# A planner that gives out shared PSUM banks when an operation begins, and counts changes between whole and tiled matmuls

## The chip, the cores and the metric

The kernel runs on one core of a Trainium2 chip. The metric is device time in microseconds (us) from launch to end; a lower number is better. A time of a kernel is the median of several runs, and a profile is one further execution in which every instruction has its start and its duration.

## The reference

```python
def _attn_ref(q, k, v, p):                     # 8 batches, 8 heads, 576 tokens, width 64
    scale = 1.0 / np.sqrt(q.shape[-1])
    def sm_attn(qq, kk, vv):
        s = scale * np.matmul(qq, kk.transpose(0, 1, 3, 2))
        s = s - np.max(s, axis=-1, keepdims=True)
        a = np.exp(s)
        a = a / (np.sum(a, axis=-1, keepdims=True) + 1e-09)
        return np.matmul(a, vv)
    p_packed = sm_attn(p, k, v)                # 32 packed rows for each head
    return sm_attn(q, p_packed, p_packed)
...
x = attn_out.transpose(0, 2, 1, 3).reshape(4608, 512)
h = x @ w_in                                   # 512 x 1024
sm = softmax(h);  solu = h * sm
ln = (solu - mean) / np.sqrt(var + 1e-06) * g_ln
x = ln @ w_out                                 # 1024 x 512
h = x @ w_in2                                  # 512 x 2048
return np.maximum(h, 0.0) ** 2 @ w_out2        # 2048 x 512
```

## The kernel before

The program has four stages, and the engines overlap them. The **attention stage** works through 16 units, numbered 0 to 15: one unit is four heads of one batch. For a unit, k and q are loaded (tiles `kr`, `qr`, which share one buffer), transposed on DVE (`kT`, `qT`), and laid out anew by DMA inside SBUF (`k2`, `q2`; units 0 to 3 use `kT` as it is). On PE a unit makes the scores of the packed rows (`s1_mm`, two halves), the transposes of their exponentials (`pt_tr`), the packed values (`pp_mm`), a transpose of these (`pp_tr`), the scores of q against them (`s2_mm`, two halves) and the product of the packed values with the first layer's input weights (`g_mm`, two halves, tile `G`). DVE, ACT and GpSimd (POOL) do maxima, exponentials, sums and copies between these steps.

The **first layer** takes 36 tiles of 128 tokens: `h` is built from `aT` (the transposed second softmax) and `G` of the batch's two units, in four steps, the softmax and norm follow on DVE, ACT and POOL, PE transposes the result (`tr`, banks `ptv`) and multiplies it with the output weights (`y_mm`, operations in two halves of 12 matmuls). The weights come in as raw double precision and are decoded on ACT, DVE and POOL while the first units run: four tiles `wi`, then four tiles `wx` that end as `wo`. The **z** and **o** stages are the second layer, whose two products are made with fewer multiplications by sums and differences of blocks; their weights are decoded and stored during the stages ahead of them (`prepare`).

All work is written down as operations with their engine, a guessed duration, the buffers they read and write, and a first urgency. A **planner** (class `Plan`) then sets the order in which each engine issues its instructions. It runs the operations through a simple model of the chip (`order`): an operation that has its inputs is *ready*, and a free engine takes the ready operation with the smallest urgency. Then `backward` runs the order from its end to its beginning and replaces each urgency by the latest time at which the operation may start. Eight such passes are made, and the last order is the program. PE, DVE, ACT, POOL and the DMA queue each carry out their list strictly in that order. Some operations may go to either of two engines, and the planner chooses (the last step of decoding, L503, is one of them).

Eight banks of PSUM exist. Four of them, the ring `m` that `bank()` hands out, are shared by every short product: scores, transposes, `pg`, `py`, and later `pw`, `pz` and `pa`. In the kernel before, `claim` gives an operation its bank as soon as it is ready, in the order in which operations become ready; an operation that finds no bank free is put into the ring's queue, and is made ready anew when a bank is returned. So a ready operation of low urgency that PE will not take for a long time holds a bank meanwhile. The planner gives each matmul operation a duration that does not depend on its neighbour.

A matmul is called *whole* here when it uses all 128 rows and columns of the array, and *tiled* when it uses 64 of the rows or columns and two or four run side by side: `s1_mm` from unit 4 on, `pp_mm`, `s2_mm`, `g_mm` (L543, L667, L713).

Of the kernel before, what the change touches and what calls it, by code (L numbers as in the profile page):

```python
# [40 lines left out]
class Ring:  # L41


    def __init__(self, tag, bufs, shared):
        self.tag, self.bufs, self.shared = tag, bufs, shared
        self.last, self.free, self.queue = [], list(range(bufs)), []
# [35 lines left out]
class Op:  # L82


    def __init__(self, engines, urgency, fn, lag, bufs, deps, port):
        self.engines, self.urgency, self.fn, self.lag, self.bufs, self.deps = engines, round(urgency, 6), fn, lag, bufs, deps
        self.port = port
        self.engine = None


class Plan:
# [5 lines left out]
    WINDOW = 3413.0  # L97

# [50 lines left out]
    def reset(self):  # L149
        for o in self.ops:  # L150
            o.engine = None
            for b in o.bufs:
                b.slot = None
                if b.ring:
                    b.ring.free, b.ring.queue = list(range(b.ring.bufs)), []

    def backward(self):
# [47 lines left out]
    def order(self):  # L205
# [7 lines left out]
        events = []  # L213
# [25 lines left out]
        order = []  # L239

        def claim(i):
            need = [b for b in ops[i].bufs if b.ring and b.ring.shared and b.slot is None]
            for n, b in enumerate(need):
                if len(b.ring.free) <= sum(c.ring is b.ring for c in need[:n]):
                    b.ring.queue.append((ops[i].urgency, i))
                    return False
            for b in need:
                b.slot = b.ring.free.pop(0)
            return True

        def take(e, t):
            nonlocal port
            while not busy[e] and able[e]:
                _, i = heapq.heappop(able[e])
                o = ops[i]
                if o.engine is not None:
                    continue
# [3 lines left out]
                if e == POOL or e == DVE and o.port:  # L261
                    port = self.span = max(t, port) + o.engines[e]
                else:
                    self.span = pe_end(t, o.engines[e]) if e == PE else t + o.engines[e]
                self.ends[i] = self.span
                heapq.heappush(events, (self.span, i, "free"))
                heapq.heappush(events, (self.span + o.lag, i, "done"))

        while events:
            now = events[0][0]  # L270
            while events and events[0][0] <= now:
                t, i, what = heapq.heappop(events)
                o = ops[i]
                if what == "ready":
                    if claim(i):
                        for e in o.engines:
                            heapq.heappush(able[e], (o.urgency, i))
                elif what == "free":
                    busy[o.engine] = False
                else:  # L280
                    for b in o.bufs:
                        uses[b] -= 1
                        if not uses[b] and b.slot is not None:
                            b.ring.free.append(b.slot)
                            for _, j in sorted(b.ring.queue):
                                heapq.heappush(events, (t + 200, j, "ready"))
                            b.ring.queue.clear()
# [4 lines left out]
            for e in (PE, ACT, POOL, DVE, DMA):  # L292
                take(e, now)
        assert len(order) == len(ops), "the plan is stuck"
# [15 lines left out]
def kernel(  # L310
# [46 lines left out]
    PASSES = 8  # L357
    SUB, KLO, ALO = (POOL,), (DVE,), (POOL,)
# [198 lines left out]
    def pack(at, b, g):  # L557
# [61 lines left out]
        for hf in range(2):  # L619
# [8 lines left out]
            plan.op(PE, c_prod(2, SH, True) if early else PAIR, at + 4, s1_mm, r=[pb, ks], w=[ps])  # L628
            plan.op(DVE, c_dve(SH), at + 5, lambda ps=ps, hf=hf: nc.vector.tensor_reduce(
# [40 lines left out]
        plan.op(PE, KJ * 280 + 60, at + 10, pp_mm, r=[eT, vr], w=[ppp])  # L670

# [20 lines left out]
    def unpack(at, b, g, packed):  # L692
# [3 lines left out]
        for hf in range(2):  # L696
# [4 lines left out]
            plan.op(PE, PAIR, at, s2_mm, r=[ppq, qs], w=[s2])  # L701
            plan.op(DVE, c_dve(SH), at + 1, lambda s2=s2, bs=slice(hf * NB // 2, (hf + 1) * NB // 2): nc.vector.transpose(
# [3 lines left out]
        for f in range(F1 // 512):  # L706
# [7 lines left out]
            plan.op(PE, 957, at + GA, g_mm, r=[ppq, wi[2 * g], wi[2 * g + 1]], w=[pg], claim=[gt])  # L714
            hi_op(at + GA + 1, 512, lambda fs=fs: gt()[:, 0, fs], pg, [pg], [gt])
# [539 lines left out]
```

## Time and profile before

| what | us |
|---|---|
| median of 3 runs | 1254.61 |
| lowest and highest of them | 1252.86, 1256.75 |
| span of the profiled execution | 1251.4 |
| PE busy in that span | 1201.0 (96%) |
| DVE, ACT, POOL busy | 894.0, 785.4, 205.3 |

For the profiled execution the span from the first to the last instruction is the only time shown; it lies 3.2 us below the median of the runs. Matmuls overlap each other by a little, so a busy PE can hide small gaps, and the start of a matmul tells more than its duration. "Idle before" names the time that an engine sat idle and what ended it.

### The profile page before, as it was taken

How to read it: one execution, taken by the hardware profiler on the slowest of the kernel's cores; microseconds unless marked ns; L12 is line 12 of the kernel's file. 1: busy time of each engine (PE TensorE's matmuls, PEld its weight loads, DVE VectorE, ACT ScalarE, POOL GpSimd, SP SyncE). 2: the span in 40 equal slices, each digit the busy share in tenths (PEclk: the TensorE clock that was granted, in tenths of full speed). 3: DMA queues.
4: the chain of work that ended last, by engine and by line, in shares of the span. 5: the costliest groups of instructions: out<-in, count | busy, mean ns of one | idle time of the engine just before them, and what ended most of it. 6: DMA issues, size and time to landing. Idle time of an engine off the chain costs nothing.

```text
span 1251.4 us, 23307 instructions
## 1 busy us (share of the span) xinstructions
PE 1201.0 (96%) x8332; PEld 1097.0 (88%) x8332; DVE 894.0 (71%) x1756; ACT 785.4 (63%) x1669; POOL 205.3 (16%) x250
## 2 busy tenths in 40 slices
PE   3769999999999999999999999999999999999998
PEld 2337887788877789999999999999999999999998
DVE  5897768575867765355686867582778797878885
ACT  2476757575856667478777877787655554545452
POOL 2274534434344442000000000000000000000000
PEclk9989999999999999999999999999999999999999
DMA  8964765765677628656867576746996535343501
GB/s 193 244 177 126 198 197 151 214 175 160 183 214 188 183 81 314 225 194 202 259 191 242 172 257 203 225 156 203 375 352 202 150 117 152 116 150 104 173 31 51
DMA packets 185240, 234.60 MB, mean 187 GB/s; under 512 B 24356, under 2 KB 148772, under 8 KB 184356
## 3 DMA queue, kind: packets, MB, share of 16 engines
q1 hardware_dynamic: 144708, 208.20, 54.4%
q10 hardware_dynamic: 40416, 24.91, 6.6%
q8 instruction: 65, 1.06, 0.4%
q14 instruction: 51, 0.42, 0.1%
HBM read 130.55 MB, written 85.98 MB: 173 GB/s over the span
## 4 chain that ended last, share of the span: by engine, by line
PE 84%; DMA 7%; DVE 4%; POOL 2%; ACT 1%; issue 1%; SPq 1%; DVEq 0%; POOLq 0%; ACTq 0%
PE px L469 10%; PE px L471 10%; PE px L470 10%; PE ph L784 7%; PE pa L469 5%; PE pa L471 5%; PE pa L470 5%; PE py L469 4%; PE py L470 4%; PE py L471 4%; PE pz L470 3%; PE pz L471 3%; PE pz L469 3%; PE ptv L827 2%; PE s L543 2%; PE pg L713 2%
## 5 line engine op out<-in xcount | busy, mean ns | idle before, releaser
L451 ACT CAST cb<-ga 128x384 fp32r<-128x384 f32 x336 | 168.3, 513 | 164.2 <-PE px L471 72.8
L454 DVE TENSOR_TENSOR cb<-ga,cb 128x384 fp32r<-128x384 f32 x336 | 181.2, 555 | 59.1 <-ACT cb L451 58.0
L469 PE MATMUL py<-v,wo 128*128 128x256 f32 x576 | 169.2, 294 | 0.7 <-DVE G L454 0.3
L470 PE MATMUL py<-v,wo 128*128 128x256 f32 x576 | 162.7, 282 | 0.0
L471 PE MATMUL py<-v,wo 128*128 128x256 f32 x576 | 162.6, 282 | 0.0
L469 PE MATMUL px<-oi,cb 128*128 128x256 f32 x504 | 142.3, 282 | 2.0 <-ACT cb L451 2.0
L471 PE MATMUL px<-oi,cb 128*128 128x256 f32 x504 | 142.0, 282 | 0.1
L470 PE MATMUL px<-oi,cb 128*128 128x256 f32 x504 | 141.8, 281 | 0.0
L469 PE MATMUL pa<-oi,cb 128*128 128x256 f32 x504 | 141.4, 281 | 0.0
L471 PE MATMUL pa<-oi,cb 128*128 128x256 f32 x504 | 141.0, 280 | 0.0
L470 PE MATMUL pa<-oi,cb 128*128 128x256 f32 x504 | 141.0, 280 | 0.0
L469 PE MATMUL px<-y,zi 128*128 128x384 f32 x384 | 129.4, 337 | 0.0
L470 PE MATMUL px<-y,zi 128*128 128x384 f32 x384 | 129.4, 337 | 0.0
L471 PE MATMUL px<-y,zi 128*128 128x384 f32 x384 | 129.3, 337 | 0.0
L469 PEld LDWEIGHTS py<-v,wo 128*128 128x128 f32 x576 | 109.7, 191 | 13.1 <-issue 9.4
L470 PEld LDWEIGHTS py<-v,wo 128*128 128x128 f32 x576 | 110.0, 191 | 0.6
L471 PEld LDWEIGHTS py<-v,wo 128*128 128x128 f32 x576 | 109.8, 191 | 0.0
L1032 DVE TENSOR_TENSOR gw<-pz,gw 128x384 f32<-128x384 f32 x96 | 53.2, 554 | 73.3 <-PE pz L471 64.0
L972 DVE TENSOR_TENSOR ga<-ga 128x384 f32<-128x384 f32 x192 | 100.4, 552 | 0.9
L469 PEld LDWEIGHTS px<-oi,cb 128*128 128x128 f32 x504 | 95.9, 190 | 2.2 <-ACT cb L451 2.2
L471 PEld LDWEIGHTS px<-oi,cb 128*128 128x128 f32 x504 | 96.0, 190 | 0.3 <-DVE cb L454 0.3
L470 PEld LDWEIGHTS px<-oi,cb 128*128 128x128 f32 x504 | 95.6, 190 | 0.0
(179 smaller groups left out, 2972.6 us busy)
## 6 DMA issues: line engine op xcount, KB each, us to landing
g_dram<-gw SPq DMA_DIRECT2D x192, 192.0 KB
ga<-g_dram SPq DMA_DIRECT2D x96, 384.0 KB
zi<-z_dram SPq DMA_DIRECT2D x28, 512.0 KB
oi<-o_dram SPq DMA_DIRECT2D x24, 512.0 KB
kr<-in_k_dram SPq DMA_DIRECT2D x16, 576.0 KB
qr<-in_q_dram SPq DMA_DIRECT2D x16, 576.0 KB
q<-qT SPq DMA_DIRECT2D x64, 144.0 KB
y_dram<-ysb ACTq DMA_DIRECT2D x72, 128.0 KB
```

Of the source, the lines that this page charges most:

```text
L451: plan.op(ACT, c_act(cols, sbuf=r[0].pool not in (psm, psh, pso)), at, lambda: nc.scalar.copy(out_(), in_()), r=r, w=w)
L454: plan.either(on(cols, *engines), at, lambda e: vec[e].tensor_tensor(out_(), in_(), hi_().bitcast(F32), op=ALU.subtract), r=r, w=w, port=i ...
L469: nc.tensor.matmul(ps, lh, rh, start=first, stop=False, skip_group_check=onto)
L470: nc.tensor.matmul(ps, lh, rl, start=False, stop=False, skip_group_check=onto)
L471: nc.tensor.matmul(ps, ll, rh, start=False, stop=last, skip_group_check=onto)
L543: nc.tensor.matmul(ps()[64 * e:64 * e + 64, :SH], cols(lhs, e), cols(rhs, e)[:, cs], start=True, stop=True)
L713: nc.tensor.matmul(pg()[es, :], ppq()[:, e], wi[2 * g + e]()[:, fs], start=True, stop=True)
L784: nc.tensor.matmul(ph()[:, fs], al[l]()[:, g], g_tiles[b, g]()[:, r, fs], start=ends[0] and g == 0 and t == 0, stop=ends[1] and g == NG - ...
L827: nc.tensor.transpose(pt()[:, c * P:(c + 1) * P], e()[:, (4 * t + c) * P:(4 * t + c + 1) * P], ident)
L972: plan.op(DVE, c_dve(cols), at, lambda: nc.vector.tensor_tensor(out_(), in0(), in1(), op=op), r=r, w=w, port=True)
L1032: plan.op(DVE, c_dve(HN), when(p, SN), lambda: nc.vector.tensor_tensor(t(), ps()[:, :HN], t(), op=ALU.add), r=[t, ps], w=[t])
```

## The change

The instructions are the same; the planner that orders them differs in four ways. A bank of the shared ring is now claimed when PE begins the operation (`claim` is called in `take`), so a ready operation holds nothing. If an operation cannot get its banks, the engine looks at the next one by urgency, and what it would have needed is held back from less urgent ones. A bank that is returned counts as free 200 ns later. And the model of PE adds 90 ns when a tiled operation follows a whole one, and 200 ns when a whole one follows a tiled one (`SWITCH`; `tiled` marks the operations). A field `slack`, which would make operations earlier in the backward pass, is added but stays 0, and `AHEAD` is not read.

```diff
+        self.slack, self.tiled = 0, False
...
+    SWITCH = {True: 90.0, False: 200.0}
...
-                    free[j] = max(free[j], t + self.hop(ops[j].engine, e) + ops[j].lag)
+                    free[j] = max(free[j], t + self.hop(ops[j].engine, e) + ops[j].lag + ops[j].slack)
...
-        def claim(i):
-            need = [b for b in ops[i].bufs if b.ring and b.ring.shared and b.slot is None]
-            for n, b in enumerate(need):
-                if len(b.ring.free) <= sum(c.ring is b.ring for c in need[:n]):
-                    b.ring.queue.append((ops[i].urgency, i))
+        mode = [False]
+
+        def claim(i, held, now):
+            need = {}
+            for b in ops[i].bufs:
+                if b.ring and b.ring.shared and b.slot is None:
+                    need.setdefault(b.ring, []).append(b)
+            for ring, bufs in need.items():
+                if sum(f <= now for f, _ in ring.free) - held.get(ring, 0) < len(bufs):
+                    for r, bs in need.items():
+                        held[r] = held.get(r, 0) + len(bs)
                     return False
...
+                if not claim(i, held if keep else {}, t):
+                    back.append(item)
+                    continue
...
+                elif e == PE:
+                    ns = o.engines[e]
+                    if o.tiled != mode[0]:
+                        ns += self.SWITCH[o.tiled]
+                        mode[0] = o.tiled
+                    self.span = pe_end(t, ns)
...
                 if what == "ready":
-                    if claim(i):
-                        for e in o.engines:
-                            heapq.heappush(able[e], (o.urgency, i))
+                    for e in o.engines:
+                        heapq.heappush(able[e], (o.urgency, i))
...
-                            b.ring.free.append(b.slot)
-                            for _, j in sorted(b.ring.queue):
-                                heapq.heappush(events, (t + 200, j, "ready"))
-                            b.ring.queue.clear()
+                            b.ring.free.append((t + 200, b.slot))
+                            heapq.heappush(events, (t + 200, i, "wake"))
...
+            plan.ops[-1].tiled = not early
```

The order moves from the first microseconds to the end of the first layer; in the z stage a few neighbours change places, and in the o stage the order of PE is the same. The lines of the changed file are 24 to 28 higher (L543 becomes L567, L784 becomes L812). Three places show it.

On **PE**, at unit 5, where the scores of q (`s<-q`) and the product with the weights (`pg`) stand between the steps of `h` (`ph`), the order before is:

```order
392 L827 MATMUL ptv<-ident,e 128x128 x4
393 L543 MATMUL s_1669<-q_1265,ppq 64x288 x2
394 L543 MATMUL s_1676<-q_1265,ppq 64x288 x2
395 L784 MATMUL ph<-G,ah 128x512 x4
396 L784 MATMUL ph<-G,al 128x512 x2
397 L543 MATMUL s_1696<-k_1432,pbz_752 64x288 x2
398 L713 MATMUL pg<-wi_327,ppq 64x512
399 L713 MATMUL pg<-wi_364,ppq 64x512
400 L784 MATMUL ph<-G,ah 128x512 x4
401 L784 MATMUL ph<-G,al 128x512 x2
```

and the order after:

```order
186 L812 MATMUL ph<-G,ah 128x512 x4
187 L812 MATMUL ph<-G,al 128x512 x2
188 L567 MATMUL s_1252<-q_1031,ppq 64x288 x2
189 L567 MATMUL s_1261<-q_1031,ppq 64x288 x2
190 L740 MATMUL pg<-wi_322,ppq 64x512
191 L740 MATMUL pg<-wi_367,ppq 64x512
192 L740 MATMUL pg<-wi_322,ppq 64x512
193 L740 MATMUL pg<-wi_367,ppq 64x512
194 L812 MATMUL ph<-G,ah 128x512 x4
195 L812 MATMUL ph<-G,al 128x512 x2
```

Here the four tiled operations of the unit stand in one run between whole ones, where before they stood in two runs, with the unit's other `pg` pair in a third further down.

On **PE**, at unit 3 (scores `s<-kT`, their transposes `pt`), while the weights are still being decoded, the order before is:

```order
38 L543 MATMUL s_547<-q_459,ppq 64x288 x2
39 L625 MATMUL s_559<-kT,pbz_142 128x288 x2
40 L761 MATMUL ph<-G,aT 128x512 x2
41 L625 MATMUL s_576<-kT,pbz_142 128x288 x2
42 L761 MATMUL ph<-G,aT 128x512 x2
43 L653 MATMUL pt<-ident,e_608 128x128 x4
44 L653 MATMUL pt<-ident,e_608 64x128
```

and the order after:

```order
38 L789 MATMUL ph<-G,aT 128x512 x2
39 L649 MATMUL s_565<-kT,pbz_142 128x288 x2
40 L649 MATMUL s_573<-kT,pbz_142 128x288 x2
41 L740 MATMUL pg<-wi_207,ppq 64x512
42 L740 MATMUL pg<-wi_222,ppq 64x512
43 L789 MATMUL ph<-G,aT 128x512 x4
44 L678 MATMUL pt<-ident,e_621 128x128 x4
45 L678 MATMUL pt<-ident,e_621 64x128
```

Between the unit's last score and its transposes there stood one step of `ph`, and now there stand an operation of `pg` and two steps of `ph`; both scores come in a row.

On **DVE**, at the decoding of the first `wx` and the attention of unit 1 (`d_504`, `d_456` are its row sums, `pp` is unit 2's), the order before is:

```order
61 L500 SCALAR_TENSOR_TENSOR wraw<-wraw 128x1024
62 L644 TENSOR_SCALAR rs<-sm 128x1
63 L503 TENSOR_TENSOR wx<-wx,wraw 128x1024
64 L646 RECIPROCAL rs<-rs 128x1
65 L726 TENSOR_REDUCE d_504<-a_443 128x18
66 L673 SCALAR_TENSOR_TENSOR pp<-ppp,rs,mask 128x256
67 L728 TENSOR_SCALAR d_504<-d_504 128x18
68 L495 SCALAR_TENSOR_TENSOR wx<-wx,wraw 128x1024
69 L729 RECIPROCAL d_504<-d_504 128x18
```

and the order after:

```order
61 L519 SCALAR_TENSOR_TENSOR wx<-wx,wraw 128x1024
62 L754 TENSOR_REDUCE d_456<-a_410 128x18
63 L669 TENSOR_SCALAR rs<-sm 128x1
64 L522 TENSOR_SCALAR wraw<-wx 128x1024
65 L756 TENSOR_SCALAR d_456<-d_456 128x18
66 L671 RECIPROCAL rs<-rs 128x1
67 L524 SCALAR_TENSOR_TENSOR wraw<-wraw 128x1024
68 L757 RECIPROCAL d_456<-d_456 128x18
69 L606 STREAM_TRANSPOSE pbz_142<-pr 32x2x32 x3
70 L699 SCALAR_TENSOR_TENSOR pp<-ppp,rs,mask 128x256
```

The `TENSOR_TENSOR wx<-wx,wraw` of L503 is no longer in DVE's list; it is POOL's now, which carries it out ahead of its multiplication with `g_neg`. The transposes for `pbz`, which stood earlier, come later.

## Rows read from the trace of the kernel before

**Rows 1.** The page: busy us, share of the span, instructions of each engine.

```profile
PE 1201.0 (96%) x8332; PEld 1097.0 (88%) x8332; DVE 894.0 (71%) x1756; ACT 785.4 (63%) x1669; POOL 205.3 (16%) x250
```

**Rows 2.** Busy time by stretch: us, engines' busy us (instructions), PE clock, DMA share, GB/s.

```profile
0.00:100.00 100.00, 59.19 (x248) 29.78 (x249) 79.55 (x130) 48.86 (x92) 41.30 (x44) 0.95 0.80 204
100.00:520.00 420.00, 417.14 (x2963) 344.01 (x2961) 288.69 (x550) 279.01 (x609) 164.05 (x206) 1.00 0.63 183
520.00:885.00 365.00, 364.29 (x2099) 363.46 (x2099) 232.54 (x459) 274.69 (x578) 0.00 (x0) 1.00 0.67 215
885.00:892.00 7.00, 4.87 (x28) 4.46 (x27) 5.59 (x12) 3.91 (x9) 0.00 (x0) 0.81 1.03 382
892.00:1247.00 355.00, 355.00 (x3001) 355.00 (x3001) 287.21 (x606) 178.88 (x383) 0.00 (x0) 1.00 0.49 158
```

**Rows 3.** What PE waited for: us in total, times, the longest.

```profile
PE s L625 <- DVE pbz L582: 10.4, 1, 10.4
PE ptp L683 <- DVE pp L673: 8.9, 2, 5.3
PE pt L653 <- ACT e L640: 8.6, 4, 3.8
```

**Rows 4.** Timeline of PE around tiled products: start us, us, line, operation, count.

```profile
161.08 0.28 PE L470 MATMUL py<-v,wo 128*128 128x256 f32 x1
161.20 0.28 PE L471 MATMUL py<-v,wo 128*128 128x256 f32 x1
161.41 1.46 PE L667 MATMUL ppp<-vr,eT 128*64 128x128 f32 x20
...
204.66 0.71 PE L543 MATMUL s<-k,pbz 128*64 128x288 f32 x4
205.19 1.03 PE L713 MATMUL pg<-wi,ppq 128*64 128x512 f32 x4
...
453.74 0.71 PE L543 MATMUL s<-q,ppq 128*64 128x288 f32 x4
454.38 0.39 PE L469 MATMUL py<-v,wo 128*128 128x256 f32 x1
454.60 0.28 PE L470 MATMUL py<-v,wo 128*128 128x256 f32 x1
```

**Rows 5.** Timeline of PE within a run of h products.

```profile
307.44 1.07 PE L784 MATMUL ph<-G,ah 128*128 128x512 f32 x4
...
308.80 1.07 PE L784 MATMUL ph<-G,ah 128*128 128x512 f32 x4
```

**Rows 6.** Timeline of DVE and POOL while weights are decoded.

```profile
41.89 0.65 DVE L487 TENSOR_SCALAR wi<-wi 128x1024 int32<-128x1024 int32 x1
...
45.87 2.38 POOL L503 TENSOR_TENSOR wi<-wi,wraw 128x1024 f32<-128x1024 f32 x1 [6.61 <-DVE wraw L500]
45.90 2.90 DVE L487 TENSOR_SCALAR wi<-wi 128x1024 int32<-128x1024 int32 x1
...
62.16 2.05 DVE L503 TENSOR_TENSOR wx<-wx,wraw 128x1024 f32<-128x1024 f32 x1
```

**Rows 7.** Timeline of PE before the transposes of unit 3.

```profile
74.80 1.88 PE L761 MATMUL ph<-G,aT 128*128 128x512 f32 x4
...
80.49 1.39 PE L653 MATMUL pt<-ident,e 128*128 128x128 f32 x5 [3.81 <-ACT e L640]
```

**Rows 8.** Timeline of SP: loads of k and q of units five and six.

```profile
109.22 0.58 SPq L438 DMA_DIRECT2D kr<-in_k_dram  x1
...
122.59 0.58 SPq L438 DMA_DIRECT2D qr<-in_q_dram  x1
...
128.99 0.35 SPq L438 DMA_DIRECT2D kr<-in_k_dram  x1
```

**Rows 9.** Timeline of PE: the first scores of units 5 and 13.

```profile
146.43 1.14 PE L543 MATMUL s<-k,pbz 128*64 128x288 f32 x8
...
377.44 0.71 PE L543 MATMUL s<-k,pbz 128*64 128x288 f32 x4
```

More of the change, by code (lines that the diff above doesn't have):

```diff
@@ L45, in __init__ @@
         self.tag, self.bufs, self.shared = tag, bufs, shared
-        self.last, self.free, self.queue = [], list(range(bufs)), []
+        self.last, self.free = [], [(0.0, n) for n in range(bufs)]
 class Pool:
@@ L154, in reset @@
                 if b.ring:
-                    b.ring.free, b.ring.queue = list(range(b.ring.bufs)), []
+                    b.ring.free = [(0.0, n) for n in range(b.ring.bufs)]
     def backward(self):
@@ L239, in order, with take @@
         order = []
-        def claim(i):
-            need = [b for b in ops[i].bufs if b.ring and b.ring.shared and b.slot is None]
-            for n, b in enumerate(need):
-                if len(b.ring.free) <= sum(c.ring is b.ring for c in need[:n]):
-                    b.ring.queue.append((ops[i].urgency, i))
-                    return False
-            for b in need:
-                b.slot = b.ring.free.pop(0)
+        mode = [False]
[8 more added lines that the diff above has]
+                        held[r] = held.get(r, 0) + len(bs)
+                    return False
+            for ring, bufs in need.items():
+                for b in bufs:
+                    b.slot = ring.free.pop(0)[1]
             return True
-        def take(e, t):
+        def take(e, t, keep=True):
             nonlocal port
+            back, held = [], {}
             while not busy[e] and able[e]:
-                _, i = heapq.heappop(able[e])
+                item = heapq.heappop(able[e])
+                i = item[1]
                 o = ops[i]
                 if o.engine is not None:
+                    continue
+                if not claim(i, held if keep else {}, t):
+                    back.append(item)
                     continue
@@ L262, in take @@
                     port = self.span = max(t, port) + o.engines[e]
+                elif e == PE:
[4 more added lines that the diff above has]
+                    self.span = pe_end(t, ns)
                 else:
-                    self.span = pe_end(t, o.engines[e]) if e == PE else t + o.engines[e]
+                    self.span = t + o.engines[e]
                 self.ends[i] = self.span
@@ L267, in take @@
                 heapq.heappush(events, (self.span + o.lag, i, "done"))
+            for item in back:
+                heapq.heappush(able[e], item)
         while events:
@@ L293, in order @@
                 take(e, now)
+            if not events:
+                for e in (PE, ACT, POOL, DVE, DMA):
+                    take(e, now, False)
         assert len(order) == len(ops), "the plan is stuck"
@@ L357 @@
     PASSES = 8
+    AHEAD = 0.0
     SUB, KLO, ALO = (POOL,), (DVE,), (POOL,)
@@ L670, in pack @@
         plan.op(PE, KJ * 280 + 60, at + 10, pp_mm, r=[eT, vr], w=[ppp])
+        plan.ops[-1].tiled = True
         pp = ab.tile([P, 2, P], F32, "pp", tag="s", bufs=2)
@@ L701, in unpack @@
             plan.op(PE, PAIR, at, s2_mm, r=[ppq, qs], w=[s2])
+            plan.ops[-1].tiled = True
             plan.op(DVE, c_dve(SH), at + 1, lambda s2=s2, bs=slice(hf * NB // 2, (hf + 1) * NB // 2): nc.vector.transpose(
@@ L714, in unpack @@
             plan.op(PE, 957, at + GA, g_mm, r=[ppq, wi[2 * g], wi[2 * g + 1]], w=[pg], claim=[gt])
+            plan.ops[-1].tiled = True
             hi_op(at + GA + 1, 512, lambda fs=fs: gt()[:, 0, fs], pg, [pg], [gt])
```

2 lines of the change are left out of this document (added).

## Prediction

> **What bounds the kernel now.** I read the page's busy times first, then the stretches, then what PE waited for. PE is busy 1201.0 of the span of 1251.4 us, the next engine, DVE, 894.0 [rows 1]. The stretches say where PE's idle 50 us lie [rows 2]: 40.8 in the first 100 us, 2.9 from 100 to 520 us (the attention stage and the first layer), 0.7 from 520 to 885, 2.1 in the seven microseconds where the z stage hands over to the o stage, none from 892 to 1247, and 4.4 us of the span lie behind that. So from 100 us on the time is the work on PE. What remains to be won is the work itself, which the change leaves the same but for the order, and the idle time of the first 100 us. There PE waited 10.4 us for the first scores' operand, 8.9 for two packed values that DVE scales, and 8.6 for four exponentials [rows 3]: DVE, busy 79.6 of these 100 us [rows 2], sets the pace, since it decodes the weights as well.
>
> The o stage keeps its order, and the z stage swaps a few neighbours whose inputs are all there. The handover at 885 us keeps its order too. All that can move the time lies ahead of 520 us.
>
> **The change, part by part.** First the **changes between whole and tiled matmuls**. What one costs is in the starts on PE [rows 4]. Two whole matmuls of `py` start 0.12 apart (161.08, 161.20), but the tiled `ppp` after them starts 0.21 later (161.41): 0.09 for going tiled. A tiled score operation takes 0.53 when a tiled one follows (204.66 to 205.19) and 0.64 when a whole one follows (453.74 to 454.38): 0.11. And the first whole matmul takes 0.22 (454.38 to 454.60) where its kind takes 0.12: 0.10. A way there and back costs 0.30, one change 0.15 on the mean. I counted them in the two orders of PE. Behind the first 55 operations, which PE has done at about 100 us, there are 117 changes before and 88 now: 29 fewer. Unit 5 shows how: four tiled operations in one run, where two runs and part of a third stood. 29 x 0.15 = 4.35, and as PE has no cover there (417.1 of 420 busy), all of it should come off: **-4.3**. In the first 55 operations there are 30 changes where 19 stood: 11 x 0.15 = 1.65 at most, and nothing where a wait follows. PE is idle 40.8% of that stretch, 8.9 us of it right behind the tiled `ppp` [rows 2, 3]; I take **+0.5**, with ends 0 and 1.65.
>
> Second, the **order in the first 100 us**. Three moves matter. At unit 3 PE waited 3.81 us for the exponentials [rows 7]; now one more step of `ph`, which took 1.88 there [rows 7], and an operation of `pg` (1.03 at 205.19 [rows 4]) stand ahead of that wait. That is up to -2.9 if they are not missed at the next wait, and 0 if they are. Nearly the same work of DVE lies ahead of PE's 55th operation in both orders (two maxima and a transpose more, one pass over `e` and L503 less), so most of it will be missed: I take -1. The last step of decoding the first `wx` (L503) leaves DVE, where it took 2.05 [rows 6], for POOL, where its like took 2.38. By DVE's list alone that is -2.05. But while POOL ran that step at 45.87, a step of DVE that takes 0.65 alone (41.89) took 2.90 (45.90 to 48.80) [rows 6]: DVE lost 2.25. So the move lies between -2.05 and +0.3, and nearer to the second, as DVE has no gaps there: 0. The first half of unit 1's scores now stands ahead of unit 0's second scores. That holds back the latter's maximum by one score, some 2 us if it takes as long as the step of `ph` with 1.88 [rows 7], but what hangs on it (`aT`, then `ph`) now comes later in PE's order too, so 0, with ends 0 and +2. Together **-1.0**, with ends -5.0 and +2.3.
>
> A page of the Trainium skill speaks against the move of L503. "SBUF — State Buffer", section "SBUF: two separate sides", says that DVE and POOL share one pair of ports under an exclusive lock, and that whoever comes second stands still for the other's whole instruction. The 2.90 us of the DVE step at 45.90 bear it out [rows 6]. By that rule alone the move would cost 2.38 - 2.05 = 0.3 us, by the list of DVE without it it would gain 2.05.
>
> Third, the **waits between 100 and 520 us**. They are 2.9 us now [rows 2], so no more than that can be won. They can grow, because attention runs ahead now. In the trace unit 5's first score starts at 146.43 and unit 13's at 377.44 [rows 9]: 231.0 / 8 = 28.9 us per unit. In the new order there stand between the same two marks 28 fewer halves of `y` (12 x 0.12 = 1.44 us each [rows 4]), 12 fewer steps of `h` (308.80 - 307.44 = 1.36 [rows 5]) 15 fewer transposes and scores (0.53 each at most, as the score at 204.66 [rows 4]) and 5 fewer `pg` (1.03 [rows 4]): 40.3 + 16.3 + 8.0 + 5.2 = 69.8, which leaves 161.2 / 8 = 20.2 us per unit. PE, DVE and ACT take their lists strictly in order, so a unit that comes late holds up the `y` behind it, which in a slower march was cover. k and q share one buffer, and from the load of unit 5's k to that of unit 6's it took 19.8 us with DVE under load [rows 8]. That fits into 20.2, but with little to spare, so I take two more microseconds of waits, **+2.0**, with ends -2.9 and +10 (eight units late by 1.2 us each).
>
> The sum is -4.3 + 0.5 - 1.0 + 2.0 = -2.8. The profiled execution has 1251.4 and would have 1248.6; it lies 3.2 below the median of the runs, 1254.6, which I move by as much: **1251.8**, 0.22% less. A measurement of this kernel can tell about 0.3%, 3.8 us, from no change.
>
> **The rivals.** *The first 100 us shrink too.* If the operations put into unit 3's wait are not missed later, and DVE does gain the 2.05 us, the opening gives 5.0, the waits further on stay at 2.9, and the time is 1254.6 - 4.3 + 0.5 - 5.0 = 1245.8. For it speaks that 40.8 us are idle there; against it that DVE's work ahead of PE's 55th operation is nearly the same, and the row of 2.90 us. *Attention's march is too fast for the shared buffer of k and q, and the time grows.* The point from which this decides is 20.2 us per unit for the chain load k, transpose, load q, transpose. If DVE reaches the transposes a little later than at unit 5, and the chain takes 21.4, eight units bring 9.6 us, and with the rest the sum is -4.3 + 0.5 - 1.0 + 9.6 = +4.8, or 1259.4; at 21.7 us per unit it is 1261.8. For it speaks that the chain took 19.8 in a stretch in which little else held it; against it that PE waited only 2.9 us in 420 before, with an order made in the same way. *The changes saved are worth nothing*, because PE then stands at the next operation for as long: the time stays at 1254.6. Against it speaks that PE is saturated; a wait of its own would have to appear at most of the 29 places.
>
> **How the numbers follow.** The forecast of about -2.8 us has 0.36. The shorter opening has 0.33, and lies below 1250.8, faster by over 0.3%. The late chain has 0.24, and lies above 1258.4. That nothing changes has 0.07. So faster 0.33, within 0.3% 0.43 (the forecast and the last rival), slower 0.24. The range of 1245 to 1262 takes in 1245.8 and 1261.8, and leaves about 1 in 10 on either side; the forecast's own range is 1250.8 to 1255.
>
> **What would show it.** Right, if from 100 us to the end of the first layer PE does the same matmuls in some 4 us less, with its waits there below 6 us. The march is right if unit 13's first score comes some 65 us earlier than at 377, with the loads of k about 20 us apart. The opening is right if PE's idle time in the first 100 us is 39 to 41 us, and the DVE steps beside POOL's new L503 are as stretched as at 45.90. Wrong would be many waits of PE of about 1 us for `kT`, `k2` or the exponentials between 100 and 330 us (the slower rival), or an opening with 4 us less idle time (the faster one). A wait at the start of the z stage, at about 515 us, would be something that I have left out.

## The result: 1.4% slower, and the profile after

The changed kernel takes 1271.6 us (median of 4 runs, 1270.8 to 1275.1); the kernel before took 1254.1 beside it (1252.9 to 1256.8). The ratio is 1.0143, with a 95% interval of 1.0127 to 1.0160. The forecast was 1251.8 with a range up to 1262, so the time lies outside the range, on the side of the slower rival. The profiled execution spans 1270.0 us, 18.6 more than before.

First the page's busy times of the changed kernel, to be read against [rows 1]:

```profile
PE 1204.9 (95%) x8332; PEld 1100.5 (87%) x8332; DVE 901.7 (71%) x1759; ACT 784.6 (62%) x1667; POOL 198.2 (16%) x247
```

PE is idle 65.1 us where it was idle 50.4, so 14.7 of the 18.6 us are idle time of PE, and 3.9 are busy time, with the same matmuls. The stretches (us, engines' busy us with instructions, PE clock, DMA share, GB/s) stand against [rows 2]; the z stage now hands over at about 905 us instead of 886:

```profile
0.00:100.00 100.00, 58.31 (x230) 28.87 (x232) 78.70 (x123) 46.82 (x87) 43.85 (x46) 0.88 0.79 204
100.00:520.00 420.00, 404.07 (x2845) 331.61 (x2846) 289.17 (x545) 269.30 (x593) 153.26 (x200) 1.00 0.60 172
520.00:904.00 384.00, 382.20 (x2234) 380.37 (x2234) 240.56 (x473) 285.71 (x597) 1.10 (x2) 1.00 0.66 217
904.00:911.00 7.00, 4.87 (x31) 4.46 (x30) 5.70 (x12) 3.80 (x9) 0.00 (x0) 0.88 1.01 374
911.00:1265.00 354.00, 354.00 (x2988) 354.00 (x2988) 287.10 (x606) 178.98 (x383) 0.00 (x0) 1.00 0.48 158
```

From 100 to 520 us PE's idle time went from 2.9 to 15.9 us: 13.0 of the 14.7 are there. The first 100 us have 41.7 idle against 40.8, and everything behind 520 us is nearly as before. The waits between 100 and 350 us (us in total, times, the longest; for PE up to 400 us) say who was late. In the changed kernel:

```profile
PE ppp L692 <- ACT eT L475: 2.9, 1, 2.9
PE py L493 <- DVE rs L671: 2.9, 2, 2.5
PE s L567 <- DMA k<-kT: 2.5, 2, 2.3
...
DVE kT L626 <- DMA z_dram<-wx: 3.6, 1, 3.6
...
DVE qT L637 <- DMA y_dram<-ysb: 2.4, 1, 2.4
DVE pT L610 <- DMA pr<-in_p_dram: 2.1, 1, 2.1
...
ACT wx L508 <- DMA w2raw<-in_moe_w_in_dram: 11.5, 4, 4.7
...
SPq L462 <- DMA y_dram<-ysb: 20.0, 10, 4.0
SPq L462 <- DMA z_dram<-wh: 15.0, 6, 4.9
...
SPq L462 <- DMA kr<-in_k_dram: 9.7, 7, 3.3
```

and in the kernel before, for the same engines:

```profile
DVE qT L613 <- DMA qr<-in_q_dram: 2.8, 2, 2.3
...
ACT wx L484 <- DMA w2raw<-in_moe_w_in_dram: 3.6, 4, 2.1
...
SPq L438 <- DMA qr<-in_q_dram: 6.0, 2, 4.1
...
SPq L438 <- DMA kr<-in_k_dram: 4.7, 4, 1.6
```

PE's own waits have no common name: a transpose, a sum, a load. One step back transfers stand out. All rows of this kind together, DVE and ACT stood 32.2 us for transfers in these 250 us (before 12.0), and SP, which issues the loads, stood 51.2 us for transfers that were still under way (before 21.5). Counting every cause, though, SP stood less than before, 112.6 us for 138.7, so its sum alone doesn't say that loads went out late. One of PE's waits, followed back through the timelines of PE, ACT and SP:

```profile
217.78 0.28 PE L495 MATMUL py<-v,wo 128*128 128x256 f32 x1
220.97 1.35 PE L692 MATMUL ppp<-vr,eT 128*64 128x128 f32 x18 [2.90 <-ACT eT L475]
...
219.89 0.66 ACT L508 ACTIVATE wx<-w2raw 128x512 f32<-128x512 f32 x1 [4.69 <-DMA w2raw<-in_moe_w_in_dram]
...
220.45 0.78 ACT L475 COPY eT<-pt 128x384 f32<-128x384 f32 x3
...
209.51 6.37 SPq L462 DMA_DIRECT2D q<-qT  x3
215.92 0.58 SPq L462 DMA_DIRECT2D vr<-in_v_dram  x1
216.55 1.42 SPq L462 DMA_DIRECT2D w2raw<-in_moe_w_in_dram  x3
```

Read from below: SP issued the first of three moves of `q` at 209.51 and in the single records the second at 214.77, so the loads of the weights `w2raw` went out between 216.55 and 217.97. ACT, which has the decoding of these weights in its list ahead of the copies `eT`, stood 4.69 us. PE, which needs `eT`, stood 2.90. In this wait the attention's own step was not late by itself; it stood behind a load in another engine's list.

The march came out near the prediction. The first scores of units 5 and 13 on PE:

```profile
123.65 0.66 PE L567 MATMUL s<-k,pbz 128*64 128x288 f32 x4
...
298.79 1.19 PE L567 MATMUL s<-k,pbz 128*64 128x288 f32 x8
```

(298.79 - 123.65) / 8 = 21.9 us per unit, where 20.2 was worked out and 28.9 stood before [rows 9]. Unit 13 comes 79 us earlier, not 65, and the loads of k are issued 21 to 22 us apart from unit 5 to unit 11.

### The profile page after: what moved, and what is told of

The parts are those of the page before. It is cut to its first block, busy times and chain, and to the rows that moved or that the text cites. A ratio compares the mean times of both kernels' runs of the same rounds, so it can differ in the third digit from the quotient of the medians.

```text
span 1270.0 us, 23307 instructions
## 1 busy us (share of the span) xinstructions
PE 1204.9 (95%) x8332; PEld 1100.5 (87%) x8332; DVE 901.7 (71%) x1759; ACT 784.6 (62%) x1667; POOL 198.2 (16%) x247
## 4 chain that ended last, share of the span: by engine, by line
PE 72%; ACT 2%; DVE 1%; DMA 1%; issue 1%; POOLq 0%; POOL 0%; ACTq 0%; DVEq 0%
PE px L493 10%; PE px L495 10%; PE px L494 10%; PE pa L493 5%; PE pa L495 5%; PE pa L494 5%; PE ph L812 4%; PE py L493 3%; PE py L494 3%; PE py L495 3%; PE pz L495 3%; PE pz L493 3%; PE pz L494 3%; PE ptv L855 1%; PE pw L494 1%; PE pw L493 1%
```

## The experiments

Three theories were in play at first. **M**, the march: attention runs ahead faster than its loads come. **S**, the charge for the changes: it leads the planner astray. **L**, luck: the old order is a good draw, and any other order loses. Two more came up on the way: **H**, the hidden reserve, and **L2**, which is luck for orders that differ as much as the changed one. The whole set in one table. PE's idle time is 400 minus PE's busy time in the profile's stretch from 100 to 500 us; the march is the time per unit from unit 5 to unit 13. The *reserve* was worked out from trace and plan: over all operations of PE between 105 and 500 us that follow without a gap (less than some 0.2 us), the real time from start to start minus the planned one (with the charge, where it is made). Positive means that PE is slower than its plan.

| kernel | median, us | ratio to before (95%) | PE idle, us | march, us | reserve, us |
|---|---|---|---|---|---|
| before | 1254.1 | 1 | 2.9 | 28.9 | +9.5 |
| changed | 1271.6 | 1.0143 (1.0127 to 1.0160) | 15.9 | 21.9 | -3.2 |
| claim_only | 1276.3 | 1.0166 (1.0146 to 1.0186) | 20.8 | 22.0 | +11.4 |
| switch_only | 1271.3 | 1.0123 (1.0106 to 1.0140) | 15.3 | 33.0 | -5.4 |
| loads_4us_later | 1272.6 | 1.0126 (1.0096 to 1.0156) | 15.1 | 24.6 | -2.0 |
| one_pass_less | 1282.6 | 1.0210 (1.0190 to 1.0229) | 22.7 | 22.7 | -1.4 |
| before_pass9 | 1258.8 | 1.0022 (1.0012 to 1.0032) | 4.3 | 29.3 | +9.9 |
| before_pass5 | 1256.7 | 1.0004 (0.9993 to 1.0016) | 4.3 | 29.1 | +10.4 |
| two_raw_buffers | 1273.9 | 1.0150 (1.0129 to 1.0170) | 19.9 | 22.9 | -4.0 |
| before_pe_faster | 1255.2 | 0.9999 (0.9984 to 1.0015) | 3.6 | 29.4 | +24.9 |
| before_pe_slower | 1264.5 | 1.0069 (1.0044 to 1.0093) | 10.4 | 31.5 | -1.8 |
| after_pe_faster | 1274.6 | 1.0135 (1.0100 to 1.0171) | 18.3 | 23.5 | +21.5 |
| after_pe_faster_loads_later | 1263.3 | 1.0065 (1.0041 to 1.0090) | 8.9 | 26.0 | +15.2 |
| after_slow_march_pe_faster | 1252.2 | 0.9962 (0.9946 to 0.9978) | 4.4 | 28.9 | +15.9 |
| switch_only_pe_faster | 1253.8 | 0.9976 (0.9963 to 0.9989) | 8.2 | 30.1 | +22.9 |
| after_same_order_more_buffers | 1270.6 | 1.0107 (1.0085 to 1.0129) | 17.7 | 22.3 | -2.2 |
| after_slow_march_alone | 1267.6 | 1.0085 (1.0070 to 1.0101) | 16.1 | 27.6 | -2.0 |
| claim_only_slow_march | 1261.7 | 1.0038 (1.0026 to 1.0049) | 6.8 | 28.5 | +6.7 |

The kernel before ran again beside each group, at 1254.9 to 1256.4 us, and the ratios are to these runs. Idle time, march and reserve are of one execution each, and it need not be a middle one: for after_slow_march_pe_faster it is the fastest of ten runs (1247.8 us), for after_pe_faster_loads_later the slowest of five (1267.4). The rows behind the idle time of the first two lines, the kernel before and then the changed one:

```profile
100.00:500.00 400.00, 397.14 (x2805) 324.50 (x2803) 281.63 (x537) 268.03 (x590) 162.95 (x204) 1.00 0.64 183
100.00:500.00 400.00, 384.07 (x2704) 312.77 (x2705) 281.03 (x531) 257.73 (x570) 150.41 (x194) 1.00 0.58 161
```

**claim_only**: the changed kernel without the charge.

```diff
-    SWITCH = {True: 90.0, False: 200.0}
+    SWITCH = {True: 0.0, False: 0.0}
```

> The changed kernel with the charge for a change between whole and tiled matmuls set to zero: only the moment at which a PSUM slot is given out differs from the kernel before. Its order lets attention run as far ahead as the changed kernel's does (unit 13's first scores are PE's operation 237, against 235 in the changed kernel and 316 before). Theory M (the march: PSUM given out late lets attention run ahead faster than k and q arrive, DVE and ACT, which take their lists in order, stand at the loads, and PE then at them): 1262 to 1276 us, with more than 10 us of PE's idle time between 100 and 400 us. Theory S (it is the charge for the changes that led the planner astray): 1250 to 1258 us, with less than 5 us idle there. Theory L (the order before was a lucky one, any other order by nearly the same rules loses as much, whatever its march): 1262 to 1276 as well, so this run tells M from S only.

1276.3 us, 20.8 us idle: as M (and L) had it, and S alone is out.

```profile
100.00:500.00 400.00, 379.17 (x2668) 308.15 (x2667) 271.86 (x529) 253.53 (x567) 150.84 (x193) 0.99 0.58 160
```

**switch_only**: the kernel before with the charge.

```diff
+                    if e == PE and o.tiled != mode:
+                        ns += self.SWITCH[o.tiled]
+                        mode = o.tiled
```

> The kernel before with the charge for the changes between whole and tiled matmuls, and PSUM given out as before, when an operation becomes ready. Attention keeps the old march (unit 13's first scores are PE's operation 336, before 316, changed 235); PE has 107 changes behind its first 55 operations and 27 within them (before 117 and 19, changed 88 and 30). Theory M: PE's idle time between 100 and 400 us below 6 us, the changes give 10 x 0.15 = 1.5 us back and the opening takes up to 1.2, so 1250 to 1258 us. Theory S: 1262 us or more. Theory L: this is another order too, so 1260 us or more with idle time spread over the stretch.

1271.3 us with the slow march. M alone is out as well: each half of the change loses by itself, and both together lose no more than one. Nor do transfers stand out here: from 100 to 350 us DVE and ACT stood 9.8 us for them (before 12.0, changed 32.2). The row from 100 to 500 us shows 15.3 us of idle time, with less traffic (0.59 DMA share) than the kernel before (0.64):

```profile
100.00:500.00 400.00, 384.67 (x2687) 310.60 (x2686) 283.11 (x533) 255.33 (x566) 152.48 (x191) 1.00 0.59 166
```

**loads_4us_later**, the same edit for `qr` (`spare` is what the planner adds to a transfer's duration before its data counts as there, 1500 ns without the edit):

```diff
-        dma(at, kr, ..., 4 * P * NB * D, w=[kr])
+        dma(at, kr, ..., 4 * P * NB * D, w=[kr], spare=5500)
```

> The changed kernel, where the planner takes the loads of k and q to need 4 us more from issue to use (some 9.3 us, where 8.6 to 11.8 us passed in the changed kernel between the issue of a load of k and its first transpose). The instructions are the same; the march is planned at 23.2 us per unit from unit 4 to unit 13 (changed kernel 20.4), PE has 19 changes in its first 55 operations and 93 behind them. Theory M: DVE no longer stands at the loads, PE's idle time between 100 and 400 us falls from some 18 us to below 8, and the opening comes back by some 3, so 1252 to 1262 us. Theory L: 1264 us or more, as for any other order. If the late loads are not the cause but PSUM or ACT is, the idle time stays above 12 us and the time above 1265.

1272.6 us: M's number missed. From 100 to 200 us the idle time did fall, from 7.8 to 2.6 us, but from 200 to 500 us it rose, from 8.1 to 12.4.

**one_pass_less**

```diff
-    PASSES = 8
+    PASSES = 7
```

> The changed kernel with one pass of the planner less: the same rules, another order of the same kind (march 20.3 us per unit in the plan, unit 13's first scores are PE's operation 235, 28 changes in PE's first 55 operations and 92 behind them; in the opening units 0 and 1 stand as before the change). Theory M: the march is the same, so PE's idle time between 100 and 400 us is again 12 to 22 us; with the opening's order nearer to the old one, 1262 to 1274 us. Theory L: the draw of an order decides, and the time may be anywhere between 1252 and 1285 us, without regard to the march.

1282.6 us and 22.7 us idle. The march's idle time came again; the time came out even longer than M had said, and lies in the range of L. Two orders by the same rules can lie 11 us apart.

**before_pass9** and **before_pass5** put L to the test: the old rules, `PASSES` at 9 and at 5.

> The kernel before with 9 passes of its planner where it has 8, nothing else: the same rules, and an order that differs little (57 neighbours of PE's list out of some 1,300 operations, none further than 5 places; the planned end is 1237.1 us against 1237.3; the march and the changes are the same, 115 for 117). Theory L (the order before is a lucky draw; any other loses the cover of single waits): slower by 3 us or more, 1258 to 1272 us, with 5 us or more of PE's idle time between 100 and 450 us. Theory M (only the march or the opening matter): 1252 to 1258 us, idle time there below 5 us.

> The kernel before with 5 passes of its planner where it has 8: the same rules, planned end 1236.9 us against 1237.3, the old march of attention (unit 13's first scores are PE's operation 317, before 316), 208 neighbours of PE's list new (changed kernel 440), 24 changes in the first 55 operations and 118 behind. Theory L: 1262 to 1275 us, about as slow as the changed kernel. Theory M: 1252 to 1260 us.

+0.22% and +0.04%, idle time 4.3 us in both. before_pass9 came out between the two theories: its 1258.8 us are at the lower end of L's range and just above M's, its idle time is M's. before_pass5, which moves more of the order, is M's in both. L falls in this form: neighbouring orders by the old rules cost 0 to 3 us, not 17.

**two_raw_buffers** (`RAW` is the third of these numbers)

```diff
-    AB, GB, RAW, TMP, VR, ET = 4, 4, 1, 2, 1, 1
+    AB, GB, RAW, TMP, VR, ET = 4, 4, 2, 2, 1, 1
```

> The changed kernel with two buffers for the loads of k and q where they share one: a load no longer waits for the transpose of the one ahead of it. The planner makes its own order for it (unit 13's first scores are PE's operation 235 as in the changed kernel, 22 changes in the first 55 operations and 92 behind). Theory M: the loads come a step earlier, DVE stops standing at them, PE's idle time between 100 and 400 us falls from 16 to below 8 us: 1256 to 1264 us. Theory L: the buffer is not the cause, 10 to 20 us of idle time there again and 1264 to 1285 us.

1273.9 us, 19.9 us idle, march 22.9. The shared buffer of k and q, on which the slower rival was built, is not what holds the march.

What switch_only and the changed kernel have in common led to H. In the kernel before the changes between whole and tiled matmuls are not planned, so PE is 9.5 us slower than its plan. The other engines are slower than theirs too: from 100 to 500 us steps of DVE that followed closely took 20 to 24 us more than planned from start to start, those of ACT 6 to 10, by whether gaps of up to 0.1 or 0.2 us count as none; where no gap at all is let through, it is 10 and 2.5. The idea: as long as PE falls behind with them, it doesn't wait, and the charge moves the plan of PE alone.

**before_pe_faster** and **before_pe_slower**, factors 0.96 and 1.04, on the planned duration of every operation of PE up to the z stage:

```diff
+    for o in plan.ops:
+        if PE in o.engines:
+            o.engines = {PE: o.engines[PE] * 0.96}
```

> The kernel before, with every operation of PE up to the z stage planned 4% shorter; nothing else changes in the rules. 384 neighbours of PE's list are new (changed kernel 440, the run with the charge alone 365), the march and the changes are about the old ones (unit 13's first scores are PE's operation 320, 24 and 118 changes). Theory H (hidden reserve: in the kernel before PE needed 9.5 us more from 105 to 500 us than planned, because the changes between whole and tiled matmuls weren't planned, and the other engines had that much time in hand for their own lateness; the charge takes it from them): PE's idle time between 100 and 450 us stays below 7 us, 1250 to 1260 us. Theory L2 (any order that differs from the old one in as many places loses, whatever its rules): 1264 to 1278 us.

> The kernel before, with every operation of PE up to the z stage planned 4% longer, some 15 us between 100 and 500 us, as much as the charge for the changes (15.2 us there); the changes themselves aren't counted and PSUM is given out as before. 319 neighbours of PE's list are new; the march is about the old one (unit 13's first scores are PE's operation 322), 23 and 115 changes. Theory H: the reserve is gone, so PE's idle time between 100 and 450 us is 10 us or more, 1262 to 1276 us. If the reserve is not the cause (it is where the charge falls, not how much time it is): below 7 us idle there, 1252 to 1260 us. Theory L2: 1264 to 1278 us, as before_pe_faster.

Ratio 0.9999 and 1.0069, idle 3.6 and 10.4 us, both as H had it. 384 new neighbours cost nothing where the reserve is larger, so L2 falls; 319 cost some 9 us (0.69%) where it is gone, without any charge. switch_only, with a reserve that is 3.6 us lower still, lost 1.23%. The two rows, first the one with PE planned faster:

```profile
100.00:500.00 400.00, 396.41 (x2801) 324.15 (x2802) 286.75 (x546) 272.64 (x598) 160.61 (x201) 1.00 0.63 176
```

```profile
100.00:500.00 400.00, 389.56 (x2713) 313.78 (x2712) 279.02 (x534) 260.37 (x578) 157.15 (x200) 1.00 0.63 176
```

**after_pe_faster** is the changed kernel with the factor 0.94, **after_pe_faster_loads_later** has in addition the edit of loads_4us_later.

> The changed kernel, with every operation of PE up to the z stage planned 6% shorter, some 23 us between 100 and 500 us, so that the planned time of PE is as much below its real one as before the change, and 10 us more. The fast march stays (unit 13's first scores are PE's operation 248 instead of 235; 21.3 us per unit in the plan). Theory H alone: PE's idle time between 100 and 400 us falls from 16 to below 7 us, 1254 to 1263 us. Theory M (late loads of the fast march): the idle time stays above 10 us, 1264 us or more. Theory L2: 1264 us or more as well.

> The changed kernel, with PE planned 6% shorter up to the z stage and the loads of k and q planned 4 us later, so both remedies at once (march 23.8 us per unit in the plan, 21 and 95 changes between whole and tiled matmuls). If the loss is made of the lost reserve and the late loads together: PE's idle time between 100 and 450 us falls below 6 us, and with an opening some 3 us slower than before 1250 to 1260 us. If neither is the cause (L2): 1264 us or more.

1274.6 and 1263.3 us. The reserve alone doesn't help the fast march, as M says; together with later loads the idle time halves, to 8.9 us. Both numbers missed, the time by 3 us and the idle time, which I had below 6. A likely reason for the time: the edit also delays the loads of units 0 to 3, and only 204 matmuls were done in the first 100 us (before 248 [rows 2]).

**after_slow_march_pe_faster** mends that, and delays the plan's loads only from unit 4 on, by 6 us; `qr` alike, factor 0.94:

```diff
-        dma(at, kr, ..., 4 * P * NB * D, w=[kr])
+        dma(at, kr, ..., 4 * P * NB * D, w=[kr], spare=1500 if early else 7500)
```

> The changed kernel with PE planned 6% shorter up to the z stage, and the loads of k and q from unit 4 on planned 6 us later (the opening's loads as they are). The plan then marches at 27.2 us per unit (kernel before 28.9, changed 20.4) and has 83 changes behind the first 55 operations (117 and 88) and 23 within them. If reserve and march together are the whole loss: PE's idle time from 100 to 500 us below 5 us, the opening within 2 us of the kernel before, and the changes saved come out as a gain of up to (117 - 83) x 0.15 = 5.1 us: 1249 to 1256 us. If a rest is left that neither explains: 1258 us or more, with 8 us or more idle.

1252.2 us, ratio 0.9962: both halves of the change, and 0.38% faster than the kernel before, as expected. The row from 100 to 500 us:

```profile
100.00:500.00 400.00, 395.65 (x2821) 329.25 (x2822) 285.06 (x544) 265.88 (x587) 148.33 (x194) 1.00 0.65 179
```

**switch_only_pe_faster** is switch_only with the factor 0.92.

> The kernel before with the charge for the changes (switch_only, 1.2% slower), and every operation of PE up to the z stage planned 8% shorter, which gives back more reserve than the charge takes. The march is the old one; 22 changes in the first 55 operations and 108 behind (before 19 and 117). Theory H: PE's idle time from 100 to 500 us falls from 15.3 to below 6 us, 1250 to 1259 us. If it is the place of the charges and not the reserve: above 10 us idle, 1262 us or more.

1253.8 us, 0.24% faster than before, where switch_only was 1.2% slower. The time is H's; the idle time, 8.2 us, is 2 more than I had said.

**after_same_order_more_buffers**: the changed kernel's lists word for word, with more room.

```diff
-            tag, bufs = self.ring.tag, self.ring.bufs
+            tag, bufs = self.ring.tag, self.ring.bufs + (self.ring.tag in ('vr', 'raw'))
```

> The changed kernel in exactly its own order on every engine, but with one buffer more in SBUF for v's loads and one more for those of k and q: a load no longer waits for the last reader of the buffer's content before it, so SP does not stand at it with the loads behind it. If the loss between 100 and 400 us comes from SP's queue standing at buffers: PE's idle time there falls from 16 to below 8 us, 1258 to 1265 us. If the loads are late because there is too much on the DMA queues, or because the lists of DVE and ACT have them at the wrong place: above 11 us, 1266 to 1274 us.

1270.6 us, 17.7 us idle: SP's queue standing at buffers is not the cause. At most a small part of the loss is left to it, as the ratio is 1.0107 where the changed kernel had 1.0143.

**after_slow_march_alone** leaves the factor out of after_slow_march_pe_faster; **claim_only_slow_march** has neither factor nor charge, so the reserve is that of the uncounted changes.

> The run after_slow_march_pe_faster without its second half: the changed kernel with the loads of k and q from unit 4 on planned 6 us later (march 26.4 us per unit in the plan), PE planned as in the changed kernel. 92 changes behind the first 55 operations, 24 within. If the lost reserve counts on its own, whatever the march: PE's idle time from 100 to 500 us is 8 us or more (after_slow_march_pe_faster about 4), 1257 to 1268 us. If the march alone is the loss: below 5 us idle, 1249 to 1255 us.

> The changed kernel with the charge for the changes at zero (claim_only, 1.7% slower) and the loads of k and q from unit 4 on planned 6 us later (march 27.1 us per unit in the plan); PE's planned times are those of the kernel before, so the reserve of the kernel before is there. 95 changes behind the first 55 operations, 25 within. If PSUM given out late costs by the fast march alone: PE's idle time from 100 to 500 us falls from 20.8 to below 6 us, 1250 to 1258 us. If the late gift of PSUM costs in another way too: above 10 us idle, 1262 us or more.

1267.6 us with 16.1 us idle: the lost reserve counts on its own. And 1261.7 us with 6.8 us idle, where claim_only had 20.8: most of what giving out PSUM late costs goes with the march, though both numbers lie above those that I gave, the time by 4 us. In its first 100 us 228 matmuls were done; that rest I have not taken apart. The first row is of after_slow_march_alone, to be read beside the one of after_slow_march_pe_faster, whose rules differ from it in the planned duration of PE's operations alone; the second is of claim_only_slow_march, to be read beside claim_only:

```profile
100.00:500.00 400.00, 383.92 (x2706) 313.67 (x2707) 282.53 (x536) 255.25 (x571) 152.53 (x191) 1.00 0.63 174
100.00:500.00 400.00, 393.22 (x2783) 322.79 (x2784) 292.05 (x544) 265.23 (x591) 154.26 (x200) 1.00 0.65 179
```

## Why the prediction was wrong

**What was shown.** Most of the loss is PE's waiting from 100 to 500 us (13.0 us of the 18.6 that the profiled execution is longer), and it has two causes, each of which is enough: the fast march and the lost reserve. The table divides by them. The eight kernels with a march of 26 us or more *and* a reserve of 6 us or more have 2.9 to 8.9 us of idle time. The other ten, which lack one or both, have 10.4 to 22.7. The two bounds were drawn after the runs, and the nearest kernels on either side are only 1.5 us of idle time apart; the pairs that differ in one rule carry more weight. The late gift of PSUM made the march fast, the charge took the reserve; that is why each half alone costs about as much as both, and why one remedy alone gave little or nothing (after_pe_faster, loads_4us_later, after_slow_march_alone) and both gave 1.8% (1.0143 to 0.9962). What is not separated: the edit that slows the march also gives every load 6 us more in the plan, so "the march" stands for both.

**The waits between 100 and 520 us** are the step that failed. I took +2.0 with ends -2.9 and +10; they measured +13.0 (15.9 for 2.9). The march was right in kind, 21.9 for 20.2, and the slower rival had its point of decision there: at 21.9 its own sum is (21.9 - 20.2) x 8 = 13.6, and -4.3 + 0.5 - 1.0 + 13.6 = +8.8, or 1263. Three things were wrong with it. Its mechanism, the shared buffer, is refuted by two_raw_buffers and after_same_order_more_buffers. Its sign for the wait, many waits for `kT`, `k2` or exponentials, was only one part: loads of weights stood late in the same queue and held ACT. For k itself did not come late: by the records of the DMA packets the last packet of k's loads ends 3.2 to 5.6 us after the issue from unit 5 on (before, units 5 to 12, 3.3 to 4.4), and DVE began the transposes no sooner than 7.6 us after it. And it counted the march alone, while the charge would have cost the same without it, which I had as no case at all. I had weighed it that PE waited only 2.9 us in 420 "with an order made in the same way" as a reason against the rival. The order was made in another way just there: the old plan was wrong about PE by 9.5 us, and that error gave the cover; with PE planned 4% longer and no other change of the rules, PE waited 10.4 us for 2.9 (before_pe_slower).

**The changes.** Their number was right: 29 fewer behind PE's 55th operation. Their price holds too, if somewhat low: in the kernel before, sorted by what stands before and behind, the half of `y` ahead of a tiled operation takes 0.16 us more from start to start than between whole ones (medians of 19 and some 80 cases), the one behind a tiled operation 0.09, and the tiled one 0.05 and 0.10. That is 0.40 there and back, 0.20 for one change, where I had 0.15. At these prices, an estimate, the changes from 100 to 520 us cost 23.7 us before and 18.6 after, so the -4.3 was there, as -5.1; in the first 100 us they cost 1.4 more, where I took 0.5. That this is what remains as a gain once the waits are gone fits after_slow_march_pe_faster, which has 106 changes in all where 136 stood, but its order differs in more than that.

**The opening.** Predicted -1.0 and an idle time of 39 to 41 us; measured 41.7. Unit 3's wait of 3.81 us [rows 7] is gone, and a new one of 5.54 stands behind it, on PE:

```profile
82.19 0.97 PE L678 MATMUL pt<-ident,e 128*128 128x128 f32 x5
83.51 1.46 PE L692 MATMUL ppp<-vr,eT 128*64 128x128 f32 x20 [0.35 <-ACT eT L475]
90.50 1.22 PE L789 MATMUL ph<-G,aT 128*128 128x512 f32 x1 [5.54 <-ACT ph L830]
```

So what was put into the wait was missed at the next one, as I had feared, and somewhat more. Only 230 matmuls were done by 100 us, for 248, at a granted clock of 0.88 for 0.95. The clock alone decides little: before_pe_faster had 0.80 there and is as fast as the kernel before. Adding up the planned times of what PE had started by then, the opening stands some 2.7 us behind. The step L503 (L527 in the changed file) on POOL (62.23, 2.40 us) held DVE less than I thought: three transposes beside it took 0.74 us together (62.36), and single ones take 0.22 (41.80) elsewhere; so DVE did gain there, and it didn't help.

The Trainium skill, "SBUF — State Buffer", section "SBUF: two separate sides", binds the lock to DVE's steps with two inputs in SBUF and to its fast modes. The three free transposes agree with it; I had applied the rule to all that DVE might do there.

**The rest**, 3.9 us more busy time in spite of the saved changes, lies largely beside the waits, by an estimate from the starts. From 100 to 520 us the operation ahead of each of PE's waits and the two behind it took some 6 us more from start to start, the wait itself left out, than the medians of their kind with the prices above (before 2 to 3). The clock adds up to 1.8 us (20 x 0.09): in the 20 us that hold PE's wait of 2.5 us for `rs`, and behind it, the granted clock (a mean of the levels 2.4 and 1.2 GHz) fell from 1.00 to 0.91.

```profile
260.00:280.00 20.00, 19.85 (x134) 15.37 (x134) 16.14 (x30) 15.17 (x35) 8.81 (x13) 1.00 0.87 220
280.00:300.00 20.00, 17.07 (x130) 15.16 (x128) 13.48 (x29) 10.37 (x24) 5.76 (x8) 0.91 0.67 195
```

**What stays open.** By which steps the fast march makes PE wait is shown for one wait of 2.9 us and argued for the others. SP's standing for transfers under way fits (51.2 us, before 21.5), but after_slow_march_pe_faster still has 36.4 and hardly waits. Nor does the time that DVE and ACT stand for transfers follow the loss: from 100 to 350 us it is 20.5 us there and 16.8 in after_slow_march_alone, whose PE waits nearly four times as long. Whether a fast march with a true picture of the transfers would do as well wasn't tried. That the other engines' lateness is what uses up the reserve is argued too; what the runs show is that planning PE faster or slower gives and takes the idle time. Nor is it known why this order of switch_only and not another waits where it does; between orders of the same kind 11 us were seen.

## What to carry to other kernels

A list that is fixed ahead of time lives from its errors as well as from its truths: where the bounding engine is planned too fast, the others have time in hand, and correcting only its price takes that time away. So plan the bounding engine a few per cent faster than it is (0.94 here, with the slower march), or correct the prices of all engines together, which wasn't tried here, and compare every engine's trace with its plan before asking what a better rule saves. And when a rule lets one stage run ahead, tell a late transfer from a late use: here 7.6 to 11.8 us passed from the issue of k to its first transpose (units 5 to 11), but its last packet was there after 3.2 to 5.6, near the 5.3 planned, and for most of the rest DVE was at other work of its list.

## What the runs showed of the hardware

In this program SP stood at DMA issues for reasons that have nothing to do with the data. In the records of the changed kernel the issues of SP and of ACT name one of eight semaphores in turn, and most issues of SP (185 of the 260 from 100 to 350 us) wait for the one that they name. The move of `q` at 214.77 waited for a store of `y` that ACT had issued at 209.94 under the same one. So a store on ACT's queue held a move on SP's, whatever the move's own inputs. How much of the 51.2 us is of this kind, and how much a wait for a buffer, I did not separate.
